# Elu features of four blocks read from the transposed q, and the order of issue written anew

## The chip, the core and the metric

The program runs on one core of a Trainium2 chip. Its time is the time of one execution on the device, in microseconds (us); the kernel before was run three times, and the median is the figure that a changed kernel is compared with. One further execution of the same program was taken by the hardware profiler; all rows below come from that one.

The engines of the core work side by side, each on its own list of instructions: PE (TensorE: matrix products, and transposes as products with the identity matrix), ACT (ScalarE), DVE (VectorE), POOL (GpSimd) and SP (SyncE, which here only issues transfers). An instruction starts when the one ahead of it on its engine is through and the data, the buffers and the transfers that it waits for are there.

## The reference

The computation is an attention with a memory branch, followed by a gated feed-forward layer:

```
scores = q k^T / sqrt(D), causal;  a = softmax(scores);  local = a v
phi(x) = (x > 0 ? x : exp(x) - 1) + 1
mem    = (phi(q) M_prev) / (phi(q) z_prev + 1e-6)
x      = g * mem + (1 - g) * local,   g = sigmoid(beta), one per head
xn     = x / rms(x) * rms_g
out    = (silu(xn w_gate) * (xn w_val)) w_out
```

q, k and v have 4 batches, 8 heads, 576 rows and 64 columns; x has 2304 tokens of 512 values; the gated layer is 1536 wide. All inputs and the output are fp32.

## The kernel before, in words

The 2304 tokens are worked off as 18 blocks of 128 rows, and the gated layer takes them as 9 chunks of two blocks. Attention of later blocks runs beside the gated layer of earlier chunks, so that TensorE always has a product to do.

The first four blocks (`n < NA`, NA = 4) take an fp32 way; the others split every operand into two fp16 halves and transpose them by DMA. Only the fp32 way is touched here. For such a block, q and k are loaded as rows (tiles `q` and `kv`, 128 rows by 512 values). `prep_qk32` transposes k and q on TensorE (`transposed`, L571: four products with `ident` into the PSUM tile `tp`), and ACT copies each 128x512 result to SBUF (L573), k into `k32`, q into the half `q32[n][:, 0]`. `phi_calc` computes phi: ACT takes the exponential of q as loaded (L553), DVE takes the smaller of that and 1 (L554), and DVE takes the larger of q + 1 and that (L555). `prep_phi32` then transposes the features `ph` in the same way (four more products at L571, one ACT copy at L573 into the half `q32[n][:, 1]`). The scores are products of `k32` and `q32[n][:, 0]` (L637); `S` is their row-reduced form on DVE (L654), its exponential is on ACT (L712), and it is transposed again on TensorE before the product with v (L852). The memory branch multiplies `q32[n][:, 1]` with a matrix `Mpair` that holds M_prev and z_prev of two heads (L825).

A block's result is put together on DVE and POOL (L838, L868, L870, tile `t`). ACT sums its squares (L428, tile `junk`), POOL makes the row's scale of it (L928, L931), DVE builds a diagonal matrix (L942, `diag`), and TensorE multiplies the block with it (L947, `xtp`), which transposes and scales at once. Two blocks make the first chunk `xT`, on which the fp32 gated products (L1105) run.

Other work of the first 60 us: `csum` (L317) sums squares of k and v for the scales of the fp16 blocks, `allp` (L289) spreads a column over all partitions, and `busy` (L308) are products whose result nobody reads; eight of them open the program. The weights come as 64-bit words and are made fp32 by ACT and DVE (L1023, L1024, L1028) and then split in fp16 halves (L245 to L266).

**What sets the order.** The order of issue of every engine is written out: `ISSUE` holds one string for each of the five engines, in which a letter stands for a kind of instruction (the letter is given by `@keep`; "T" is a transposition, "f" an operation of `phi_calc`), a number behind it for a repetition, and `~` with a number for how many of the kind that are still to come are passed over. A function reads the strings and ties each instruction to the one ahead of it. The transfers of SP are in such a string too. A transfer takes one of eight lanes in turn, and waits for the transfer eight before it.

Of the kernel before, what the change touches and what calls it, by code (L numbers as in the profile page):

```python
# [90 lines left out]
        "3SG2P2SPG~1P2G~1G~1P2S~2G~1G~1G~1PS~2PS~2S~2G~1G~1PS~2G~1D~2GPSDP~1SPSGSG5SDG3D~3GPD~3GP3DPD~2S32GDPG~2PGP3GDPGP"
        "2GP2GPD~3P3G3DG6PG2D~2PGDGPDG3PG3D~1PG~1G~1G~1P3GP2GPGP2G4P2G3YG3PG2P2D~1P3GG~6GP3GDG3G~1GPD~1D2S~8S~8S~8S~8S~20"
        "S~20S~8S~8S~8S~8S~8S~8S~8S~8S~8S~8S~8S~8S~8S~8S~8S~8S~8S~8S~8S~8S~8S~8S~8S~8S~8S~8M4S8M12P2G2PG6DG3G~11G3G~8G8D~"
        "3GDG7D~2G2S27D2G2D~1GDGG~8G2G~6G4G~2GD~2G~1G~1G~1G~1D2G~1G~1G~1G~1G~1DG2D~1GDG3PS2P2SP2G3D~2GDD~1DSPS3P3SPSPSP3S"
        "PS2P45S~8S~8S~8S~8S~8S~8S~8S~8S~8S~8S~8S~8S~8S~8S~8S~9S~9S~9S~9S~9S~9S~9P3S~9P2S~9P2S~9P2S~9S~9P4S~9P2S~9PS~8PS~"
        "8P2S~8P11G3D~1D~1G9DG15D~1D~1G4DM16P29S8GD~1G4D2G16D~1G2D~1G4D~1GS~8S~8G5S7PSG5S2GSGS~3GDSG~3G~3SG~3G~3G~3G~3GG~"
        "2G~2S~1SGDSDG5D~1GDS2GDS~3DGD~3GS~3S~3SDSDGSDG~7G2G~5DG~5G~5G2G~3SG~3G~3G~3GG~2D~1GSGS2GDS~1D~2S~1G3SDGS2P120G~1"
        "0GG~9D~1G~9G3D~1D~4D~4GG~5G3G~2G~2G~2GG~1GDMGDGD~2G10SG2G~2GG~1G~1G~1SG~1MG~1GSMSDGMDG3DG2M3GMG6MGMGG~3MG~3MG2G~"
        "1PG2M2G3P2GDGP2DP3MP2GPMDP3G3PD~2GDG3DGP2DP3GPG~5D~1G~5GPG2G~2P~2P~2P~2P~2PG~2P~1G~2P~1G~2G~2P~1P~1P~1G~2GPGD~1G"
        "PG2P2DGPG3PG3D~1PG2D2PG2P2D~1PG~2PGPG7P3SD~1G3S~5G4D~1G4DGDG~5G2S~5SS~4G3S4D~2D~2GSDGS2G4DG2SG2SGDS2M2SGSDGMD~2M"  # L100
        "S2GSM~4M~4MGMSG2SGMSG2D~2SM~1GG~2M~1M~1D~2G~2G3D2MGSS~4S2G2DS~2MGS~2DGSG2S2D~1G6DSG2PGDGS~1SGPG2P2GP4GSGSPSMSMG4"
        "P5GS~1S~1PS~1PG3SGDGPD~3G7DG3PG2S~3S~3S~3G4SPS~2GS~2GS~2G2PGPSS~1PDD~1SP2GD~1PG2PGPG3P4DPGSD~3SPSG2PSDSG3P2SGSG~"
# [66 lines left out]
def attn_memory_moe_kernel(  # L169
# [1154 lines left out]
    for n in range(2):  # L1324
        prep_qk32(n)
        phi_calc(n)
        prep_phi32(n)
# [223 lines left out]
```

## Time and profile before

| What | us |
| --- | --- |
| three runs, lowest / median / highest | 584.06 / 584.78 / 584.83 |
| the profiled execution | 583.54 |
| its span (first to last instruction) | 581.8 |
| around the span | 1.74 |
| PE busy in the span | 574.0 |
| DVE / ACT / POOL busy | 424.2 / 398.3 / 131.3 |

The profiled execution is 1.24 us below the median of the three runs. The rows further down show its views: a page of shares, the waits of an engine, its busy time in stretches of the span, and timelines, where several instructions of one kind that follow each other stand in one row with their count.

### The profile page before, as it was taken

What the parts mean: (1) busy time and instruction counts of PE and PEld (TensorE: products, weight loads), DVE (VectorE), ACT (ScalarE), POOL (GpSimd) and SP (SyncE); (2) the same over time, 40 slices, a digit from 0 to 9 for tenths busy, and PEclk for the clock granted to TensorE, in tenths of its full rate; (3) what the DMA queues carried; (4) which work ended last, traced back from release to release, by engine and by line L of the source; (5) the groups of instructions that cost most, each with busy time, mean ns of one, the idle gap of its engine ahead of it and who ended that gap; (6) DMA issues with size and microseconds to landing.
All of it is one profiled execution on the core that took longest, in us unless ns stands there. A gap on an engine that the chain in (4) does not pass through costs nothing.

```text
span 581.8 us, 16060 instructions
## 1 busy us (share of the span) xinstructions
PE 574.0 (99%) x6230; PEld 454.1 (78%) x6230; DVE 424.2 (73%) x1278; ACT 398.3 (68%) x857; POOL 131.3 (23%) x219
## 2 busy tenths in 40 slices
PE   8999999999999999999999999999999999999996
PEld 8888866687777787887777778787877777777885
DVE  5898869999997878775788787988766675642221
ACT  6899888998996757665677678867655553543222
POOL 2511100053322222212213221213221211132111
PEclk9999999999999999999999999999999999999999
DMA  8999666579898778977579877597666653462001
GB/s 260 347 361 373 238 230 130 111 133 241 168 164 156 155 158 131 148 142 138 99 160 162 175 149 155 107 180 138 111 123 114 103 100 65 95 90 47 27 1 37
DMA packets 183948, 87.59 MB, mean 151 GB/s; under 512 B 165824, under 2 KB 166080, under 8 KB 183872
## 3 DMA queue, kind: packets, MB, share of 16 engines
q1 hardware_dynamic: 180800, 81.95, 66.3%
q10 hardware_dynamic: 3072, 4.61, 2.3%
q8 instruction: 49, 0.80, 0.6%
q14 instruction: 27, 0.22, 0.1%
HBM read 37.77 MB, written 4.72 MB: 73 GB/s over the span
## 4 chain that ended last, share of the span: by engine, by line
PE 93%; DMA 3%; ACT 1%; DVE 1%; issue 0%; POOL 0%; ACTq 0%; POOLq 0%
PE gv L1112 42%; PE out L1193 21%; PE gv L1105 7%; PE sc L648 5%; PE out L1182 3%; PE loc L770 2%; PE loc L771 1%; PE loc L772 1%; PE csum L317 1%; PE sc L677 1%; PE loc L788 1%; DMA kv<-in_qkv_dram 1%; PE tp L571 1%; PE mem L886 1%; DMA q<-in_qkv_dram 1%; DMA PT<-P 1%
## 5 line engine op out<-in xcount | busy, mean ns | idle before, releaser
L1112 PE MATMUL gv<-xT,wgv 128*128 128x256 f16 x2304 | 357.1, 273 | 0.0
L1112 PEld LDWEIGHTS <-wgv 128*128 128x128 f16 x2304 | 209.2, 98 | 49.9 <-issue 3.2
L1193 PE MATMUL out<-wo,h 128*128 128x512 f16 (+1 forms) x528 | 176.0, 372 | 0.0
L1151 POOL TENSOR_TENSOR h<-th,h 128x256 f16<-128x256 f32 x88 | 64.6, 735 | 275.1 <-ACT h L1150 252.5
L1129 ACT ACTIVATE th<-gv,wt 128x256 f32<-128x256 f32 x96 | 45.1, 469 | 75.5 <-PE gv L1112 70.3
L648 PE MATMUL sc<-kT,qT 128*128 128x128 f16 x576 | 95.3, 219 | 0.0
L720 ACT ACTIVATE S<-S,nm 128x384 f32<-128x384 f32 (+3 forms) x112 | 70.7, 637 | 28.3 <-DVE nm L654 16.5
L1130 DVE SCALAR_TENSOR_TENSOR th<-th,gv 128x256 f32<-128x256 f32 x96 | 40.0, 417 | 62.0 <-ACT th L1129 61.5
L739 DVE SCALAR_TENSOR_TENSOR P<-S,P 128x512 f16<-128x512 f32 (+2 forms) x96 | 65.2, 680 | 22.3 <-ACT P L219 21.4
L654 DVE CUSTOM_DVE_ANT_0 S<-sc,mask,qsc 128x256 f32<-128x256 f32 (+2 forms) x96 | 57.8, 612 | 17.7 <-PE sc L648 16.5
L1193 PEld LDWEIGHTS <-h 128*128 128x128 f16 x564 | 54.1, 98 | 14.1 <-POOL h L1151 0.5
L219 ACT ACTIVATE P<-S 128x512 f16<-128x512 f32 (+2 forms) x96 | 58.2, 607 | 8.1 <-DMA PT<-P 6.8
L648 PEld LDWEIGHTS <-qT 128*128 128x128 f16 x576 | 52.1, 98 | 10.5 <-issue 0.6
L772 PE MATMUL loc<-v,PT 128*128 128x65 f16 x288 | 53.0, 193 | 0.0
L770 PE MATMUL loc<-v,PT 128*128 128x65 f16 x288 | 52.5, 193 | 0.4 <-DMA PT<-P 0.4
L1150 ACT CAST h<-th 128x256 f16<-128x256 f32 x88 | 34.8, 396 | 26.3 <-DVE th L1133 12.1
L771 PE MATMUL loc<-v,PT 128*128 128x64 f16 x288 | 52.5, 193 | 0.0
L1133 DVE SCALAR_TENSOR_TENSOR th<-th,wt,gv 128x256 f32<-128x256 f32 x96 | 45.6, 475 | 1.6
L1105 PE MATMUL gv<-xT,wgv 128*128 128x256 f32 x192 | 46.5, 385 | 0.0
L1105 PEld LDWEIGHTS gv<-xT,wgv 128*128 128x128 f32 x192 | 35.0, 190 | 8.3 <-issue 3.6
L770 PEld LDWEIGHTS <-PT 128*128 128x128 f16 x288 | 28.1, 98 | 6.9 <-DMA PT<-P 0.7
L886 PE MATMUL mem<-M,phT 128*128 128x65 f16 (+1 forms) x256 | 32.9, 194 | 0.0
(225 smaller groups left out, 908.4 us busy)
## 6 DMA issues: line engine op xcount, KB each, us to landing
kv<-in_qkv_dram SPq DMA_DIRECT2D x40, 256.0 KB, 3.6
q<-in_qkv_dram SPq DMA_DIRECT2D x18, 256.0 KB, 3.6
wo<-in_moe_w_out_dram SPq DMA_DIRECT2D x8, 512.0 KB, 5.1
out_dram<-res ACTq DMA_DIRECT2D x16, 256.0 KB, 2.5
wgv<-in_moe_w_val_dram SPq DMA_DIRECT2D x7, 512.0 KB, 7.2
wo<-in_moe_w_gate_dram SPq DMA_DIRECT2D x7, 512.0 KB, 7.4
qT<-qT SPq DMA_DIRECT2D x28, 128.0 KB, 2.6
wgv<-in_moe_w_gate_dram SPq DMA_DIRECT2D x5, 512.0 KB, 6.1
```

Source lines behind the costliest of these rows:

```text
L219: got = fn(*p, **k)
L648: nc.tensor.matmul(t[:, g * w + j * P : g * w + (j + 1) * P], qT[n][:, t2, h, :], kT[blk_of[(b, j)]][:, h, :], start=(t2 == 0), stop=(t2 = ...
L654: nc.vector.tensor_tensor_reduce(out=s[:, g * w : (g + 1) * w], in0=t[:, g * w : (g + 1) * w], in1=mask[:, m0 : m0 + w], scale=qsc[n][:, 5 ...
L720: nc.scalar.activation(v_, v_, AF.Exp, bias=nm[:, g : g + 1], scale=-1.0)
L739: m = nc.vector.scalar_tensor_tensor(out=p16[:, w : 2 * w], in0=s[:, :w], scalar=PSCALE, in1=p16[:, :w], op0=ALU.mult, op1=ALU.subtract)
L770: nc.tensor.matmul(a, phi_, vhi, start=(j == 0), stop=False)
L771: nc.tensor.matmul(a[:, :D], phi_, vlo, start=False, stop=False)
L772: nc.tensor.matmul(a, plo, vhi, start=False, stop=(j == nb - 1))
L1105: nc.tensor.matmul(o, wgv[:, 1 + p, o0 : o0 + P], xT[0][:, cc, at], start=(cc == 0), stop=(cc == NC - 1))
L1112: nc.tensor.matmul(o, lhs, xT[c][:, rhs, :], start=(cnt == 0), stop=(cnt == 3 * NC - 1))
L1151: nc.gpsimd.tensor_tensor(h16[:, 1], th, h16[:, 0], ALU.subtract)
L1193: nc.tensor.matmul((o if half is None else o[half])[:, at], lhs, rhs[:, at], start=(f == 0 and rhs is whi and lhs is hh), stop=(f == NF - ...
```

## The change

`phi_calc` reads the transposed q that already lies in `q32[n][:, 0]` and writes the features straight into `q32[n][:, 1]`, for the first four blocks. `prep_phi32` is gone, with its transposes and copies. The other blocks compute as before. The five strings of `ISSUE` are replaced (one pair of lines shown, of some 100).

```diff
     "DVE": (
-        ".~1f2.JZI~4Z.f2S3.~1I~4SII~3.S2IS2IS3TISiS2TiSi~1Su~1uiuiu~1uTi2Iiu~1Tiuiuiu2RiR2JfZft.ZU~1RS3USf2STSu~1SI~1iuSi"
+        ".~1J.Z.2I~4fI~4ZI.fS6.SI~3fIS2IfTS3IS2i~3SiSTiu2iuiu~1uTi2Tiu3Ii3u2RiU~1R2JZtZRfS2fS3TSIS2iu~1tuiufu2Si~1SiTSifS"
...
     @keep("f")
     def phi_calc(n):
-        ph = sb.tile([P, HD], F32, tag="t2", name="ph", bufs=1)
-        nc.scalar.activation(ph, qst[n], AF.Exp)
+        if n < NA:
+            q, ph = (q32[n][:, t].rearrange("p c s -> p (c s)") for t in range(2))
+            qst.pop(n)
+        else:
+            q, ph = qst[n], sb.tile([P, HD], F32, tag="t2", name="ph", bufs=1)
+            qst[n] = ph
+        nc.scalar.activation(ph, q, AF.Exp)
         nc.vector.tensor_scalar(ph, ph, 1.0, None, op0=ALU.min)
         nc.vector.scalar_tensor_tensor(
-            out=ph, in0=qst[n], scalar=1.0, in1=ph, op0=ALU.add, op1=ALU.max
-        )
-        qst[n] = ph
+            out=ph, in0=q, scalar=1.0, in1=ph, op0=ALU.add, op1=ALU.max
+        )
...
-    @keep("n")
-    def prep_phi32(n):
-        transposed(q32[n][:, 1], qst.pop(n), T32[2] == "a")
...
-            st[4].append((0.3, lambda: prep_phi32(n)))
...
-        prep_phi32(n)
```

On ACT the program begins, before, with the small transfers, the load of the activation table and the exponential of q of block 0 as loaded (`few` and `zz` are rms_g and z_prev; `q_104`, `q_109` are q of blocks 0 and 1 as loaded, `q_0_161` and `q_1_185` their transposed tiles):

```order
L1204 DMA few<-in_moe_rms_g_dram 128x4
L1206 DMA zz<-in_z_prev_dram 64x32 x2
L553 ACT_TABLE_LOAD
L553 ACTIVATE ph<-q_104 128x512
L1203 DMA beta_sb<-in_beta_dram 128x8
L428 ACTIVATE junk,zq<-zz 128x32
L573 COPY k_0_154<-tp 128x512
L573 COPY q_0_161<-tp 128x512 x2
L553 ACTIVATE ph<-q_109 128x512
```

Now the same place reads (the numbers of lines and tiles are those of the changed kernel, in which `q_1_178` is the tile of block 1):

```order
L1205 DMA zz<-in_z_prev_dram 64x32
L1203 DMA few<-in_moe_rms_g_dram 128x4
L1205 DMA zz<-in_z_prev_dram 64x32
L1202 DMA beta_sb<-in_beta_dram 128x8
L427 ACT_TABLE_LOAD
L427 ACTIVATE junk,zq<-zz 128x32
L576 COPY k_0_154<-tp 128x512
L576 COPY q_0_161<-tp 128x512
L557 ACTIVATE q_0_161<-q_0_161 128x512
```

The exponential of block 0 has moved behind the two copies, the table load stands ahead of the sum of squares of `zz`, and of the two copies into `q_0_161` one is left.

On DVE, between the first small operations and the first reduction of scores (`S`), stood before:

```order
L293 TENSOR_REDUCE vmax<-allp 128x1
L331 MEMSET few 128x2
L554 TENSOR_SCALAR ph<-ph 128x512
L555 SCALAR_TENSOR_TENSOR ph<-q_109,ph 128x512
L654 ISA S,nm<-sc,mask 128x128
```

and ahead of these the two operations of block 0. Now there stands:

```order
L275 TENSOR_SCALAR pw<-vmax 128x1
L558 TENSOR_SCALAR q_0_161<-q_0_161 128x512
L276 TENSOR_SCALAR pw<-pw 128x1
L292 TENSOR_REDUCE vmax<-allp 128x1
L1219 TENSOR_SCALAR gsig<-gsig 128x8
L337 COPY tmask<-mask 128x128
L559 SCALAR_TENSOR_TENSOR q_0_161<-q_0_161 128x512
L653 ISA S,nm<-sc,mask 128x128
```

Block 0 has its two operations right ahead of the first reduction; those of block 1 follow behind it, between the reductions, and the copy into `tmask`, which followed the third reduction, is ahead of the first.

On PE, after the first scores, stood before:

```order
L637 MATMUL sc<-k_0_154,q_0_161 128x128 x6
L308 MATMUL busy<-ident 128x128
L571 MATMUL tp<-ident,ph 128x128 x2
L825 MATMUL mem_315<-Mpair,q_0_161 128x130
L571 MATMUL tp<-ident,ph 128x128
```

and now:

```order
L636 MATMUL sc<-k_0_154,q_0_161 128x128 x6
L316 LDWEIGHTS kv_106
L316 MATMUL csum_615<-kv_106 128x128
L316 LDWEIGHTS kv_106
L316 MATMUL csum_615<-kv_106 128x128
L824 MATMUL mem_301<-Mpair,q_0_161 128x130
```

The transposes of `ph` are gone from the list, and so is the `busy` product of this place; there are nine instead of eight at the start. All in all PE issues 16 matmuls fewer, DVE as many operations as before. From about 100 us on PE's list is nearly the same.

## Rows read from the trace of the kernel before

**Rows 1.** The page: busy time, share of the span and instructions of each engine

```profile
PE 574.0 (99%) x6230; PEld 454.1 (78%) x6230; DVE 424.2 (73%) x1278; ACT 398.3 (68%) x857; POOL 131.3 (23%) x219
```

**Rows 2.** The page: the chain that ended last, shares of the span

```profile
PE 93%; DMA 3%; ACT 1%; DVE 1%; issue 0%; POOL 0%; ACTq 0%; POOLq 0%
```

**Rows 3.** The waits of PE inside the program: total us, times, longest us

```profile
...
PE xtp L947 <- DVE few L1214: 0.7, 1, 0.7
PE allp L289 <- ACT junk L428: 0.4, 1, 0.4
PE loc L770 <- DMA PT<-P: 0.4, 1, 0.4
```

**Rows 4.** Busy us in stretches: PE, PEld, DVE, ACT, POOL, then PEclk, DMA share, GB/s

```profile
10.00:15.00 5.00, 5.00 (x42) 4.31 (x41) 4.42 (x37) 4.87 (x22) 0.89 (x3) 1.00 1.01 373
15.00:20.00 5.00, 5.00 (x49) 4.95 (x48) 4.84 (x23) 3.68 (x17) 1.50 (x3) 1.00 1.05 408
...
26.00:40.00 14.00, 13.98 (x116) 12.60 (x117) 12.70 (x58) 13.63 (x42) 3.46 (x8) 1.00 1.03 371
120.00:130.00 10.00, 10.00 (x97) 8.16 (x95) 10.00 (x35) 9.75 (x23) 6.53 (x10) 1.00 1.00 166
...
570.00:582.00 12.00, 6.97 (x54) 4.96 (x51) 2.28 (x5) 2.92 (x6) 1.62 (x3) 0.90 0.16 46
```

**Rows 5.** All instructions of line 571: ns min/median/max, first and last start in us

```profile
L571 PE MATMUL tp<-ident,ph x16: 272/273/283, 6.8 to 33.8; 128*128 128x128 f32 x16
```

**Rows 6.** Timeline of PE: start, us, line, count, and in brackets the wait ahead

```profile
1.47 3.79 PE L308 MATMUL busy<-ident 128*128 128x128 f32 x16 [1.47 <-POOL ident L325]
...
5.05 1.06 PE L571 MATMUL tp<-ident,kv 128*128 128x128 f32 x4
...
5.90 0.37 PE L571 MATMUL tp<-ident,q 128*128 128x128 f32 x1
...
26.02 1.16 PE L947 MATMUL xtp<-diag,t 128*128 128x128 f32 x8 [0.67 <-DVE few L1214]
...
27.24 0.60 PE L571 MATMUL tp<-ident,ph 128*128 128x128 f32 x4
...
27.67 0.27 PE L571 MATMUL tp<-ident,kv 128*128 128x128 f32 x1
...
32.55 0.49 PE L571 MATMUL tp<-ident,ph 128*128 128x128 f32 x3
```

**Rows 7.** ACT's copies of transposed tiles into q32, 0 to 40 us: busy us, mean ns

```profile
L573 ACT COPY q<-tp 128x512 f32<-128x512 f32 x8 | 4.6, 574 | 1.3 <-PE tp L571 1.3
```

**Rows 8.** Timeline of ACT in the head

```profile
2.46 1.28 ACT L553 ACT_TABLE_LOAD   x1 [2.46 <-issue]
4.47 0.63 ACT L553 ACTIVATE ph<-q 128x512 f32<-128x512 f32 x1 [0.73 <-DMA q<-in_qkv_dram]
...
5.42 0.23 ACT L428 ACTIVATE junk<-zz 128x32 bf16<-128x32 f32 x1 [0.32 <-DMA zz<-in_z_prev_dram]
...
6.14 0.59 ACT L573 COPY k<-tp 128x512 f32<-128x512 f32 x1 [0.40 <-PE tp L571]
```

**Rows 9.** Timeline of DVE up to the evacuation of block 1

```profile
8.69 0.43 DVE L554 TENSOR_SCALAR ph<-ph 128x512 f32<-128x512 f32 x1 [0.46 <-ACT ph L553]
9.16 0.69 DVE L555 SCALAR_TENSOR_TENSOR ph<-q,ph 128x512 f32<-128x512 f32 x1
10.24 0.29 DVE L654 CUSTOM_DVE_ANT_0 S<-sc,mask 128x128 f32<-128x128 f32 x1 [0.40 <-POOL Mpair L812]
...
10.88 0.34 DVE L338 COPY tmask<-mask 128x128 bf16<-128x128 bf16 x1
...
22.07 0.42 DVE L868 TENSOR_TENSOR t<-loc,den 128x256 f32<-128x256 f32 x1
```

**Rows 10.** Timeline of POOL: the sum that ends block 1

```profile
21.88 1.42 POOL L870 TENSOR_TENSOR t<-t,t 128x256 f32<-128x256 f32 x2 [0.44 <-DVE t L838]
```

**Rows 11.** The waits of ACT between 60 and 150 us, for one weight's transfers

```profile
ACT wo L1024 <- DMA wo<-in_moe_w_out_dram: 2.2, 2, 1.9
```

More of the change, by code (lines that the diff above doesn't have):

```diff
@@ new lines @@
+        "uT2Su~1u2h3TG2ThG2sTGs~4s~4ss~3s2s~1sTG10h2G14ZG3shs3ZG3hG2s~4s~4G2sG~1G6s~3sGss~1s6s~3s2s~1s~1ss~1s~1s~1ss~1Gs~"
+        "1s3s~4s~4s~4s~4s4G2g2g~30g~30g38G3G~3Gg3g~19g~19gg~18g~18g~18g~18g2g~16g~16g~16g~16g2g~14g~14g9g~5g~5g5ZZ~1G~2G~"
+        "2GG~1g~18g~18g7g~11g~11g~11g~11g~11g~11g10g~1g~1gZ2Gg4g~18g~18g~18g~18g~18gg~17g~17g~17gg~16g~16g~16g~16g2g~14g~"
+        "14g~14g~14g~14g~14g6g~8g51G4ZDZ~1D~1g2D~2ZD~3DG5DG2ZG3D~2D2G5D~1DG3DG2DG4DG3DG5D~1D~2G2DG4SG16S~7GS~7DSS~6DSS~5S"
+        "GS4GDG13SG5S3G2M~8M3M~5MM~4D~1MG~3M~3M~3G~3G~3MSM~2G~3GSGSG~1G~1G~1GSG2SGSM~2G8SDSMG3SGS3G10SGS3G5M~1MG4DG8SG6SG"
@@ new lines @@
+        "S3GS2G5SG7P6G~2GP3G~1P2G~1GZPGS3G2P4S2P5GS2G4P2G9PGS~1SGG~2G~2G~2SGG~1G4SG8S2G3S2GS6MS2MGP5G~4PG~4G~4MG~4M2PMSP3"
+        "G~4PG2PG~2G~2GG~1G~1G~1GMP4DP4GMP3G2PD~2G7DGD~1G2D~1DD~3GDSDD~1DMDG2MG6M2G4DS~5G2P2GPGPGP2MPGDS~5D~1PSS~4S2S~2GP"
+        "G~5P3DS~2G~5S2DGDGM2D~3G~3GMSG~2SG~2P7SG~2P2D2PSG~2PGG~1G~1G~1G~1D~1S2G~1S~1GD~1DG4D~3G3S~1S~1DSGP~1P~1SP~1SP~1G"
+        "P~1P~1P~1GP~1P~1DP~1GP~1DP~1D~2SG~1PGSP2DP6GP2DSD~2GSGD~2G2D~2G3P2GSDGD2D~2G3MD~2SMG2M2G2S~1S~1D2MS~1D~1MDG~6G~6"
+        "SMGG~5G3MSG~2G~2G~2G~2G4D~2GMD~2D~2G2MGMS2M2GS2DP3G2PMDP2D~3PG2PMP4G2P3DGPGD~2PDSPDG2D2P7MPD~2S~3PS~3S~3DS~3DSD2"
@@ new lines @@
+        "P6S~2SS~1P2SPDD~2G7SG13S~5DG4S2GSG4S~2D~1S~2D2GS~2G4P2GP3S~2PG3SD~3G4DGPSPGDD~1D~1PDG~4P4GP3S~1G~3S~1G~3G~3GG~2G"
+        "~2S~1GSG~1G~1G~1G~1G~1DG~1GPSG2S~2PGSGD~2DG4D~1SG~4G~4G~4G~4G~4G~4M2G~4GG~3MGG~2P2G~2P3MPMG~2MG~2PD~1G~2S~5G~2P3"
+        "G~2G2MPG2D~4MPGP2GP3GPSGDSDGD~2G~2SGDSGS~1GS2MG3D~1GDG3P2D~3GSPS~2P3D~3G~14S~2PGP2G4PSG~9G2MPD~3MP2G3S~1GS~1GS~1"
+        "P2DMG~2G~2MSG~2PG~2G~2G~2MG~2PG~2SDG~2G~2G~2GG~1G~1G~1PG~1DG~1G~1GMGP2MD~3GD~3P2SD~3SDPGPDGPG~1G~1PS2G~1G~1G~1G~"
+        "1G~1SDSGPGD~3GPG2S3GSG2SG2PG2PDD~2PS~1PSDPG2G~4GPG2D2GDP~2PP~1P~1S2P~1P~1P~1GSP~1G3PS2GS3G2S2G5DD~1G3PGPG4S2D~1D"
@@ new lines @@
+        "~4G2D~4G2DG2DG~8G~8GG~7GG~6GG~5G~5GG~4G~4G~4GDGD~2GD~1D~6G~1G2DD~2D~2DG3D~2G2D~2GDG~7G~7GDG~6G~6GD~3D2G~5G~5GG~4"
+        "G~4GG~3D~3GG~2D~1G~2D~1G~2GD~1GD~1G11D2G5D~2G2DD~3D~3DG4DG4D~1DG~10G10D2D~1D~1DD~1D~1G5DG4DG6D~3GDG~7G~7D~2DG2G~"
+        "5G2D~1G4D2G2D~2G8G~10GG~9G~9D~2G~9G~9GG~8G~8GG~7G~7G~7G~7GG~6D2G~6G2G~4G~4G~4DG~4G~4D~6G~4G6DD~2D2D~2D~2D3G3D~2G"
+        "3DG10DD~5G~11D~5G~11DG~11GD~1G~10GG~9G5G~4G~4GG~3DG~3G~3G~3D~3D~2G~3G~3GG~2G2DG10D~6D~6D2D~4D~1D2D~1D~1D3D~2D~2D"
+        "~3DD~2D~1D~5D~1D~4DD~4D~4D~4D~3D3"
@@ L158 @@
     ),
     "SP": (
[L160 to L163 removed]
+        "blml2bm2W~1ml~2lWbd2lW~4dd~1W~7bW~4d~1d2a4W2dWl~1W~1lWW~2lW~1Wa4WW~2W3W~2B~6WW~1blW2B~2WB~1B4XB3XbB2rkr~1rkbkFrk"
@@ L164 @@
+        "r2l~1L2lbFll~1L2rl~1Lr2kLll~1L2FXLlLlbrlL2Xr2kL2FL2rl2L2bLr2LkXLlLlFLbLrL2rLXLrlkL2FL3lLrLbXL2m~1r~1rl~1lkLmLFL4"
+        "XrLr~1rkl~1lkL4bFLl2L2bLrkl2r~1rXFbrLXLr2kLlLlm2LFL5bL3XrL2k2r2LbFr3kL2XFL4rLbLr~1rLkLXL2FrLrL2XrL3kL2FL8X2D2"
     ),
```

152 lines of the change are left out of this document (64 added, 88 removed).

## The prediction

> **What bounds the kernel now.** I read the page's shares first. PE is busy 574.0 of 581.8 us [rows 1], and the chain that ended last is PE for 93% [rows 2]; so time goes only where PE has less to do or waits less. Of the 7.8 us in which PE is idle, about 1.5 lie ahead of its first product [rows 6] and 5.0 in the last 12 us, which the change does not touch (12.00 less 6.97) [rows 4]. Between these, the waits of PE leave 1.5 us: 0.7 and 0.4 just ahead of `xtp` of block 1, and 0.4 in the middle of the program [rows 3]. The reader is to see two stretches. Up to `xtp` of block 1 at 26.02 the head is a chain through several engines, whose end PE awaits; behind it PE is full (13.98 of 14.00) [rows 4], and what is taken off PE there comes off the end.
>
> **What is removed.** Sixteen transposes of `ph` go [rows 5]. A record lasts 273 ns, but that is a latency: four of them began at 27.24 and the next product at 27.67 [rows 6], so each takes 0.43 / 4 = 0.108 us of PE. In the head the pace is half that: four transposes of k began at 5.05 and the next at 5.90, 0.213 each [rows 6], but there PE also awaits what it transposes. All sixteen are worth 16 x 0.108 = 1.73 us if PE waits nowhere for anything else. The Trainium skill, "TensorE: Matmul & The Clock Gate", Part 4, gives about 275 ns for a transpose in a kernel's context and says it does not keep the clock up as a product does; its 275 ns is the trace's record of 273, but the trace's spacing of 108 ns says that they overlap, and the clock granted beside them is 1.00 [rows 4], the higher level of 2.4 GHz. By the rule's price taken in full the sum would have 4.4 us in this place.
>
> Eight of the sixteen (four at 27.24, three at 32.55, the last at 33.8) stand behind `xtp` [rows 5, 6], where PE is full: 8 x 0.108 = **-0.86**.
>
> The four copies into `q32` that go are 4 x 574 ns = 2.3 us of ACT [rows 7]. Two lie between 26 and 40 us, where ACT is busy 13.63 of 14.00, but PE there awaits nothing [rows 4], so I take 0 for them; their worth is bounded by 0 and the 0.4 us that PE waits at a later place for a transfer that ACT's work precedes [rows 3].
>
> **The ninth filler.** One `busy` product goes from about 10 us to the start. Eight of them take 3.79 us, 0.47 each [rows 6]. Where it stood it took PE's time too, so its move costs between 0 and 0.47. Ahead of the first transpose PE would wait for k anyway, so I stay near the lower end: **+0.06**.
>
> **The head, up to `xtp` of block 1.** Here the other eight transposes go, and the features are moved behind the transposed q. Before, the table load ran from 2.46 for 1.28 us, under the wait for q; the exponential began at 4.47, the sum of squares of `zz` at 5.42 when `zz` landed, and the copy of k at 6.14 [rows 8]. Now the sum of squares is the first that needs the table, and the load stands behind the same wait: about 5.35 + 1.28 = 6.63, then the sum of squares (0.32 to the next instruction) to 6.95. So the copy of k begins at 6.95, 0.8 later than before; copy of q at 7.5, exponential 8.0 to 8.6 (0.63 [rows 8]), and DVE's two operations (0.43 + 0.69 [rows 9]), with three small ones between them, to about 10.2. The wait at the load holds ACT's queue: the copies of k and q behind it, so the first scores on PE, so the first reduction on DVE. That reduction began at 10.24 before, 0.40 after DVE's list ahead of it was through, a wait that the row puts down to POOL's copies into `Mpair` [rows 9]; now I get 10.3. The slip of the copies is hidden because two of DVE's operations, block 1's (0.43 + 0.69 = 1.12), no longer stand ahead of it.
>
> The Trainium skill, "ScalarE: Activation LUTs", "What ACT_TABLE_LOAD costs", adds a drain of about 1380 ns to a load of 1283. The trace has the load at 1.28, and the exponential started 0.73 after it, at the landing of q [rows 8], so a drain of 1.38 is not seen. By the rule the copies would begin 1.4 later still, and the head would lose what the sum has it gain.
>
> Those 1.12 us of block 1 now lie among the reductions, and the copy of `tmask` (0.34) leaves [rows 9]: DVE has 0.78 us more to do between 10.24 and the evacuation of block 1, which ended at 22.07 + 0.42 = 22.49 [rows 9]. Its idle time there is 0.58 in 10 to 15 us and 0.16 in 15 to 20 [rows 4], 0.74 together. From 22.49 to `xtp` at 26.02 it is 3.5 us over POOL's sum (to 23.30 [rows 10]), ACT, POOL and DVE, all of them untouched. What PE's side gives: PE is busy 5.00 of 5.00 in both stretches [rows 4], so with its eight transposes gone (0.86) it hands scores and transposes to DVE earlier.
>
> The bounds for `xtp` of block 1: if DVE's added work comes on top of everything, 0.78 later; if PE sets the pace and its 0.86 is passed on, and the two waits of 0.4 and 0.7 go as well, 0.86 + 1.1 = 1.96 earlier. PE and DVE are both nearly full here, so neither is the whole truth. If only one of the two paces counts at a time, the middle of 0 (added work just fills the idle) and -0.86 is the nearest to both rows: **-0.4**.
>
> **The sum.** -0.86 + 0.06 - 0.4 = -1.2 us. The profiled execution took 583.54, which would become 582.3; it lies 1.24 below the median of the runs, 584.78, which becomes **583.6**. (About 0.2%, 1.17 us, is what a measurement of this kernel can tell from no change; this forecast stands on that border.)
>
> **The rivals.**
>
> *The head gives everything.* PE's eight transposes in the head come off in full, and the waits of 0.4 and 0.7 go as far as the new order lets `xtp` come earlier. For it: PE is at 5.00 of 5.00 from 10 to 20 us. Against it: both waits end on ACT, POOL and DVE [rows 3], whose work is not less. -1.7 (all transposes) to -2.8 (with both waits): 583.1 to 582.0, about 582.4.
>
> *The head swallows it.* DVE's added 0.78 us is on the path, `xtp` is 0.8 later, and the 0.86 behind it only makes up for that: -0.1, so 584.7. For it: DVE is at 4.84 of 5.00 from 15 to 20 us [rows 4]. Against it: it has 0.74 of idle time to take it up. A table load with a drain would lead to the same place.
>
> *Slower, in the weights' stretch.* SP's list of transfers is new as well, and a transfer waits for the one eight before it. DVE is busy 10.00 of 10.00 us between 120 and 130, ACT 9.75 [rows 4], and PE already waits 0.4 for a transfer of P behind it [rows 3]. ACT once waited 1.9 us for a weight `wo` in 60 to 150 us [rows 11]. If one more such weight lands late by as much, ACT's conversion and then DVE's full list slip by 1.9, and what was gained ahead is awaited away: +1.9, 586.7. It decides from the point where the weight is later than ACT's 0.25 us of slack in that stretch. Against it: from 100 us on the order is nearly as before, and a head that is earlier gives the transfers no less time.
>
> *Transposes at their full latency.* If TensorE did nothing else beside them, 16 x 0.273 = 4.4 us go: 580.4. Against it is the spacing of 0.108; for it only the 0.213 of the head. The page of the Trainium skill named above (TensorE, Part 4) speaks for this one.
>
> That the change doesn't do what it says I see no room for: the transposes are gone from PE's list.
>
> **How the numbers follow.** The forecast (its own range 582.9 to 584.2) has 0.45, half of it over the border of 0.2% and half within. The head gives everything: 0.22; it swallows: 0.22; slower in the weights' stretch: 0.09; full latency: 0.02. Faster by over 0.2% is then 0.23 + 0.22 + 0.02 = 0.47, within 0.2% is 0.22 + 0.22 = 0.44, and slower 0.09. The range 582.0 to 585.3 leaves out the last two rivals and allows for half a microsecond on the one that swallows.
>
> **What would show it.** Right: 64 records of `tp` on PE and four copies of q and four of k on ACT; the table load at about 5.3 and the copy of k at 6.9; the first reduction of scores at 10.2 to 10.4; `xtp` of block 1 at 25.3 to 25.9, and what follows it (the first fp32 gated products) earlier by 1.0 to 1.4; the same 0.4 us wait of PE for P near 130 us, or a longer one. The forecast is wrong in the head if `xtp` comes at 26.5 or later, or at 24.5 or before; it is wrong later if PE shows a new wait behind 60 us of more than half a microsecond, and its end is then to be read from what that wait ends on.

## The result: slower, 588.77 us for 584.81

The changed kernel takes 588.77 us (median of 4 runs, 588.05 to 589.61), the kernel before, measured beside it, 584.81 (584.06 to 585.02): ratio 1.0065 [1.0052, 1.0078], 4.0 us slower. The forecast was 583.6, its range ended at 585.3. The two profiled executions stand 5.3 us apart in time and span (588.82 and 587.1, for 583.54 and 581.8). Some runs of these kernels show a lower granted clock and are several us longer; the ratios leave out the two longest (595.55 in h2, 595.77 in f4, of the table below) and hold the others.

The changed kernel's page, first the shares and then the chain that ended last:

```profile
PE 575.1 (98%) x6214; PEld 452.3 (77%) x6214; DVE 425.6 (72%) x1278; ACT 397.3 (68%) x853; POOL 126.5 (22%) x219
...
PE 78%; DVE 12%; DMA 5%; ACT 2%; issue 2%; POOL 0%; ACTq 0%; DVEq 0%; POOLq 0%
```

The 16 matmuls are gone, but DVE, 1% of the chain before [rows 2], is now 12% of it. The waits of PE in the changed kernel (total us, times, longest):

```profile
PE allp L288 <- ACT junk L427: 1.5, 2, 1.3
...
PE gv L1111 <- DVE th L1132: 1.3, 1, 1.3
PE xtp L946 <- DVE few L1213: 0.7, 1, 0.7
PE loc L769 <- DMA PT<-P: 0.6, 1, 0.6
```

Against [rows 3] two are new in size: 1.3 us in the head, at the sum of squares of `zz`, and 1.3 at a gated product that awaits DVE's `th`. The second stands at 129 us, a hundred microseconds behind everything that the edit of the features touches (the order of issue is new there too). The wait for `PT`, P as a transfer transposes it, is new in place: 0.56 us at 173 us, where the kernel before waits 0.43 at 132. The stretches show it (busy us of PE, PEld, DVE, ACT, POOL; PEclk, DMA share, GB/s), before:

```profile
120.00:150.00 30.00, 29.57 (x326) 24.13 (x324) 29.77 (x98) 27.68 (x59) 14.57 (x24) 1.00 0.96 198
150.00:180.00 30.00, 30.00 (x325) 22.38 (x323) 29.26 (x84) 27.15 (x57) 8.22 (x11) 1.00 0.90 162
```

and after:

```profile
120.00:150.00 30.00, 28.03 (x302) 22.63 (x300) 29.96 (x92) 25.95 (x56) 11.94 (x17) 1.00 0.86 170
150.00:180.00 30.00, 29.29 (x312) 21.17 (x309) 28.77 (x79) 27.11 (x58) 7.60 (x12) 1.00 0.88 165
```

In the first stretch DVE is busier than before (29.96) and yet gets through fewer instructions: 92 for 98. So some of them last longer. DVE's timeline in the changed kernel, with the two POOL operations that matter:

```profile
126.57 1.16 POOL L268 TENSOR_TENSOR wgv<-wgv 128x512 f16<-128x512 f32 x1 [3.44 <-ACT wgv L265]
126.61 1.67 DVE L738 SCALAR_TENSOR_TENSOR P<-S,P 128x512 f16<-128x512 f32 x1
...
137.82 1.16 POOL L268 TENSOR_TENSOR wgv<-wgv 128x512 f16<-128x512 f32 x1 [0.20 <-ACT wgv L265]
138.35 0.65 DVE L279 TENSOR_SCALAR qsc<-pw 128x2 f32<-128x2 f32 x1
```

And before, the same instructions:

```profile
125.18 0.68 DVE L739 SCALAR_TENSOR_TENSOR P<-S,P 128x512 f16<-128x512 f32 x1
125.30 1.57 POOL L269 TENSOR_TENSOR wgv<-wgv 128x512 f16<-128x512 f32 x1 [3.32 <-ACT wgv L266]
...
135.30 0.14 DVE L280 TENSOR_SCALAR qsc<-pw 128x2 f32<-128x2 f32 x1
135.34 1.16 POOL L269 TENSOR_TENSOR wgv<-wgv 128x512 f16<-128x512 f32 x1
```

`P` takes 0.68 us where it starts 0.12 before POOL's operation, which then takes 1.57 for 1.16; it takes 1.67 where it starts 0.04 behind it. An operation on 128x2 elements goes from 0.14 to 0.65. In these pairs whoever starts second waits out the first. No wait of PE behind 60 us ends on POOL in the changed kernel; DVE is full, and there it costs time. I call the sum over DVE's instructions between 110 and 160 us of what each lasts beyond the median of its operation and operands (where over 0.12 us) the *stretch*: 0.36 us before, 3.27 after, from 6 instructions. The Trainium skill, "GPSIMD Engine Reference" (specifications), says that GpSimd shares SBUF interfaces with VectorE and contends with its instructions that have two SBUF inputs or are in a two-port mode; `P`, with two operands in SBUF, is such a case, and the trace agrees that they collide.

The other new wait is in the head. ACT, DVE and PE in the changed kernel:

```profile
6.21 1.28 ACT L427 ACT_TABLE_LOAD   x1 [6.21 <-DMA zz<-in_z_prev_dram]
7.50 0.23 ACT L427 ACTIVATE junk<-zz 128x32 bf16<-128x32 f32 x1
7.73 0.57 ACT L576 COPY k<-tp 128x512 f32<-128x512 f32 x1
7.88 0.49 PE L288 MATMUL allp<-ident,zq 128*128 128x128 f32 x2 [1.30 <-ACT junk L427]
11.11 0.29 DVE L653 CUSTOM_DVE_ANT_0 S<-sc,mask 128x128 f32<-128x128 f32 x1
27.33 0.94 PE L946 MATMUL xtp<-diag,t 128*128 128x128 f32 x6 [0.72 <-DVE few L1213]
```

The load does wait for `zz`, as forecast, but `zz` landed at 6.13 us and not at 5.34: SP now issues the first transfer of `M_prev` 2.2 us earlier (1.70 for 3.93), and `zz`, issued at 2.02, lands 0.17 behind it.

To tell where time is lost I use one mark: the 193rd gated product (`gv`) on PE, up to which both programs issue the same ones. It starts at 107.9 us before and at 108.7 after, so 0.8 of the 5.3 us of the profiled pair is lost ahead of it and **4.5 behind it**.

### The profile page after: what moved, and what is told of

The parts are those of the page before. It is cut to its first block, busy times and chain, and to the rows that moved or that the text cites. A ratio compares the mean times of both kernels' runs of the same rounds, so it can differ in the third digit from the quotient of the medians.

```text
span 587.1 us, 16001 instructions
## 1 busy us (share of the span) xinstructions
PE 575.1 (98%) x6214; PEld 452.3 (77%) x6214; DVE 425.6 (72%) x1278; ACT 397.3 (68%) x853; POOL 126.5 (22%) x219
## 4 chain that ended last, share of the span: by engine, by line
PE 78%; DVE 12%; DMA 5%; ACT 2%; issue 2%; POOL 0%; ACTq 0%; DVEq 0%; POOLq 0%
PE gv L1111 37%; PE out L1192 18%; PE gv L1104 5%; PE sc L647 4%; DMA PT<-P 3%; DVE S L653 2%; PE csum L316 1%; PE sc L676 1%; PE loc L787 1%; PE loc L769 1%; DVE wgv L247 1%; PE loc L770 1%; DVE P L738 1%; PE loc L771 1%; PE loc L851 1%
## 5 line engine op out<-in xcount | busy, mean ns | idle before, releaser
L1192 PE MATMUL out<-wo,h 128*128 128x512 f16 (+1 forms) x528 | 173.7, 372 | 0.0
L719 ACT ACTIVATE S<-S,nm 128x256 f32<-128x256 f32 (+3 forms) x112 | 70.6, 640 | 38.4 <-DVE nm L653 25.9
L647 PE MATMUL sc<-kT,qT 128*128 128x128 f16 x576 | 94.1, 219 | 0.3 <-DVE nm L653 0.3
```

Of the source, the lines that this page charges most:

```text
L647: nc.tensor.matmul(t[:, g * w + j * P : g * w + (j + 1) * P], qT[n][:, t2, h, :], kT[blk_of[(b, j)]][:, h, :], start=(t2 == 0), stop=(t2 = ...
L719: nc.scalar.activation(v_, v_, AF.Exp, bias=nm[:, g : g + 1], scale=-1.0)
L1192: nc.tensor.matmul((o if half is None else o[half])[:, at], lhs, rhs[:, at], start=(f == 0 and rhs is whi and lhs is hh), stop=(f == NF - ...
```

## The experiments

The theories: *A*, the head (the table load behind `zz`) makes the kernel slower; *B*, the new order of issue between 105 and 200 us does; and within B, *B1*, DVE's instructions that fall behind POOL's, or something else of the order. Each table row gives the median, the ratio to the kernel before that was measured beside it, and from the profiled execution its time, the start of the mark, the lag gathered behind it (mark to end, less 473.9 of before), the stretch, and the time from the 421st to the 601st gated product, which lie at 153 and 194 us in the kernel before.

```
run                    us      ratio [95%]              profile mark   lag   stretch 421-601
after                  588.77  1.0065 [1.0052, 1.0078]  588.82  108.7  +4.5  3.27  42.73
e1_early_table         587.61  1.0037 [1.0019, 1.0055]  585.92  107.9  +2.3  1.80  42.61
e2_square_first        590.02  1.0095 [1.0057, 1.0134]  586.51  110.0  +0.8  1.60  40.93
e3_edit_alone          590.06  1.0086 [1.0072, 1.0100]  591.03  113.2  +2.2  1.60  40.93
e4_thin_before         585.93  1.0012 [1.0001, 1.0022]  586.04  108.6  +1.8  0.00  40.93
e4_thin_after          587.17  1.0045 [1.0024, 1.0066]  589.27  110.0  +3.6  0.00  42.43
h1_tail_before         586.92  1.0051 [1.0021, 1.0081]  589.67  111.9  +2.1  1.60  40.94
h2_tail_before_early   586.01  1.0021 [1.0012, 1.0030]  586.02  108.6  +1.8  1.60  40.94
f1_M_back              587.40  1.0041 [1.0028, 1.0054]  588.56  108.0  +4.9  3.22  42.93
f2_M_back_early        588.08  1.0055 [1.0043, 1.0067]  588.40  108.0  +4.8  3.21  42.98
f3_M_back_early_tail   586.68  1.0041 [1.0021, 1.0061]  588.42  110.4  +2.3  1.61  40.94
f4_tail160_before      589.02  1.0059 [1.0040, 1.0078]  589.72  109.2  +4.9  3.23  41.92
g1_swaps               586.46  1.0017 [1.0008, 1.0026]  586.53  108.3  +2.6  0.40  42.09
g2_after_swaps         586.43  1.0026 [1.0015, 1.0037]  588.87  111.0  +2.3  0.41  42.60
g3_best                584.94  1.0005 [0.9994, 1.0017]  584.73  108.3  +0.8  0.77  40.94
g4_k1_early            585.21  0.9999 [0.9989, 1.0009]  585.21  107.9  +1.7  0.78  40.94
```

The profiled execution is one of several, and its time can stand 3.5 us from the median. In those of h1, f3, g2 and e3 the granted clock fell to 0.50 ahead of the mark, so their marks are late by that as well; lags are counted from the mark.

**The table load taken from behind `zz`.** In the changed kernel one more exponential of a column stands ahead of it on ACT:

```
+        early = tiny.tile([P, 1], F32, tag="early", name="early", bufs=1)
+        keep("*")(nc.scalar.activation)(early, ident[:, 0:1], AF.Exp)
```

> The changed kernel with one more instruction: ACT takes the exponential of one column of the identity matrix right behind its four small transfers, so that the activation table is loaded at about 3 us and no longer behind the landing of z_prev at 6.2. Theory H (the head: the load behind z_prev makes the copy of k, the first reduction and all of DVE's list late, and the stretch in which DVE is full, 90 to 160 us, hands it on): copy of k at about 6.5 in place of 7.73, first reduction of scores at 10.0 to 10.3 in place of 11.11, xtp of block 1 at 26.0 to 26.5 in place of 27.3, and 1.0 to 1.7 us less in all, about 587.4. Theory C (DVE's instructions of 110 to 160 us are stretched where a POOL instruction starts just ahead of them, 3.3 us in the changed kernel against 0.4 before): the head comes earlier as H says, but the time follows the stretching, which the shift deals anew: between 583.5 (none left) and 588 (all left). Rival R (the new order between 26 and 120 us is what costs): head earlier, time within 0.5 us of the changed kernel's 588.8.

The load went to 3.23 us, the copy of k to 6.42, the first reduction to 10.41, the mark to 107.9, level with before. The kernel gained 1.2 us of the 4.0 in its median; it stayed slower. Its lag also fell, to 2.3, though nothing of the order behind 105 us had been touched: an earlier head shifts when DVE and POOL meet, and in the profiled execution fewer met (it is a short one: 585.92, of runs from 585.76 to 588.55).

**The reverse: the kernel before with the square of `zz` ahead of its exponential** (ACT's list):

```
-L553 ACT_TABLE_LOAD
+L428 ACT_TABLE_LOAD
+L428 ACTIVATE junk,zq<-zz 128x32
 L553 ACTIVATE ph<-q_104 128x512
 L1203 DMA beta_sb<-in_beta_dram 128x8
-L428 ACTIVATE junk,zq<-zz 128x32
```

> The kernel before with one instruction of ACT moved: the sum of squares of z_prev goes ahead of the exponential of block 0, so that here too the table load waits for z_prev. All else is as before, the sixteen transposes too. Theory H: the load starts at 5.4 in place of 2.46, the exponential at about 7.0 in place of 4.47, the copy of k at about 7.6 in place of 6.14, the first reduction 1.0 to 1.5 later than 10.24, and 1.0 to 1.7 us more in all, about 586.1. Theory C: the same start, and on top of it up to 3 us where the shift lets POOL's instructions start ahead of DVE's in 110 to 160 us: 586 to 589. Rival R: the head's slip is taken up by PE's idle time and DVE's waits before 60 us, within 0.4 us of 584.8.

The head lost 2.1 us (first reduction 12.41, mark 110.0), more than the changed kernel's 0.8. The runs spread from 586.5 to 595.0: in four of the six the mean granted clock was 0.984 to 0.993, in the other two (586.51 and 588.40) 0.998 or more. So the median is no price of a late load; by these two it is 1.5 to 3.4 us.

**The edit in the order of before**, with the early load:

> The edit of the features alone, in the order of the kernel before: the sixteen transposes and four copies are taken out of the lists of PE and ACT, the operations of the features stand at the first place behind the copy of q that they now need, and the table is loaded early by an exponential of one column in the place of block 0's. POOL's and SP's lists are those of before. Theory H: no late load, so the head isn't late (first reduction at 9.9 to 10.4, xtp of block 1 at 25.3 to 26.5) and the time is at or under the kernel before's: 583.5 to 584.8. Theory C: the same, and up to 3 us more if POOL comes first in 110 to 160 us. Rival E (the edit itself costs, because the features follow the copies and their DVE operations come among the reductions): first reduction on time, xtp of block 1 later than 26.5, and 1 us or more above 584.8.

Inconclusive for the edit. The head was early (reduction 10.07, `xtp` of block 1 at 25.81), but PE then waited 1.0 us at 36 us for `den` of DVE, and behind it the granted clock fell to its lower level:

```profile
34.00:38.00 4.00, 2.97 (x23) 2.47 (x23) 3.66 (x23) 3.59 (x14) 0.59 (x1) 0.94 1.01 393
38.00:42.00 4.00, 4.00 (x20) 3.77 (x21) 2.07 (x9) 2.88 (x12) 0.00 (x0) 0.50 0.91 353
```

PEclk is 0.50 from 38 to 42 us, that is 1.2 GHz, behind the stretch in which PE was busy 2.97 of 4.00. All five runs have a mean clock of 0.992 or 0.993. The slow clock and the awaited DVE together put the mark 5.3 us late. In the order of before, then, the edit itself makes a wait ahead of 40 us; what it does in a fitting order these runs must tell.

**POOL's part made thin.** The low halves that POOL writes are cut to 16 columns, in before and after alike (ACT's copy writes both halves; so the low halves are not computed):

```
+            nc.scalar.copy(h16, th.unsqueeze(1).to_broadcast([P, 2, 2 * P]))
+            nc.gpsimd.tensor_tensor(h16[:, 1, :16], th[:, :16], h16[:, 0, :16], ALU.subtract)
```

> The kernel before with POOL's share of the splits made thin: in 5 splits of weights and the 8 splits of h16e, POOL computes 16 columns of the low half, and ACT's copy, which writes the high half, writes both halves. The low halves are left out of the result so. POOL then has no long instruction between 110 and 160 us that could start ahead of one of DVE's. It is the partner of the next run. Theory C (POOL's instructions stretch DVE's): little to gain here, as only 0.36 us of stretching was seen: within 1 us of 585.0. Theory O (the order of DVE's list behind 105 us): the same.

> The changed kernel with the same thin splits (the low halves of 5 splits of weights and of the 8 splits of h16e are left out of the result). Theory C: the 3.3 us of stretched DVE instructions between 110 and 160 us go, and the changed kernel stands 1.0 to 1.8 us above its thin partner (the late head alone) instead of 4. Theory O: the stretching was not what cost; it stands 3 to 4.5 us above its thin partner as without the thinning.

POOL's operation then takes 0.22 us:

```profile
129.34 0.22 POOL L270 TENSOR_TENSOR wgv<-wgv 128x16 f16<-128x16 f32 x1 [4.91 <-ACT wgv L265]
```

The stretch is 0.00 in both, and the gap of the medians is 1.24 us instead of 3.96 (1.9 by the ratios). So some half of the loss or more needs POOL's long operations. The thinning is not free itself: with it the kernel before takes 1.1 us more. The two profiled executions are 3.2 us apart: 1.4 at the mark, 0.4 more up to the 421st gated product, where the changed kernel had lost 2.7, and 1.5 from there to the 601st.

**The order of before behind 105 us**, the changed kernel's ahead of it, without and with the early load:

> The changed kernel with the order of before behind 105 us: what each engine had issued in the kernel before by 105 us comes first, in the order that the changed kernel gives it, and all the rest follows in the order of the kernel before. The late table load stays. Theory O: only the late head is left, 1.0 to 1.7 us above before: 586.0 to 586.8. Theory C: the head's delay stays, and POOL and DVE meet as it falls: 586 to 589, with stretched DVE instructions of more than 1 us in 110 to 160 us where it is above 587. Theory H in its strong form (the late head alone makes all of the 4 us): 588 to 589.

> The same as the last one with the table loaded early, as in the run that loaded it behind ACT's small transfers (587.6). Theory O: nothing of the 4 us is left, and what PE is spared behind the first chunk's xtp shows: 584.0 to 585.2. Theory C: 584 to 588, by how much DVE is stretched between 110 and 160 us. If it is 587 or more with little stretching, the loss lies in the order between 26 and 105 us.

The lag fell from 4.5 to about 2, the stretch to 1.6; with the early load as well the kernel stood 1.2 us over before. By the medians and the lags the order behind 105 us thus has a large part of the loss, though not all; the ratio of h1 is too wide to tell. Even with before's own order there, operations meet, since the head brings DVE and POOL to it at other times. In this variant:

```profile
136.08 1.16 POOL L260 TENSOR_TENSOR wgv<-wgv 128x512 f16<-128x512 f32 x1 [0.19 <-ACT wgv L257]
136.39 0.92 DVE L271 TENSOR_SCALAR qsc<-pw 128x2 f32<-128x2 f32 x1
```

Two elements in each partition, 0.92 us.

**`M_prev` back behind k and q of block 1 on SP**, and three more from there: with the early load, with the order of before behind 105 us, and (without the early load) with it only behind 160 us:

> The changed kernel with SP's first eight transfers in another order: k and q of block 1 ahead of the first part of M_prev, as before. Theory M (the transfer of M_prev, issued at 1.70 us just ahead of the second half of z_prev at 2.02, holds z_prev back: both land together, at 5.96 and 6.13 in the changed kernel, at 6.6 to 6.9 in three variants, while z_prev lands at 5.34 to 5.50 where M_prev is issued after it): z_prev lands at 5.3 to 5.5, the table load starts then, the copy of k at about 6.9 in place of 7.73, the first reduction at 10.2 to 10.5 in place of 11.11, and 0.6 to 1.2 us less in all, about 587.9. Rival D (z_prev is late because it is issued third on ACT, not because of M_prev): z_prev at 6.0 or later, no gain in the head, 588.3 to 589.2.

> The last one with the early table load as well. Theory M: the head is then as early as the kernel before's: copy of k at 6.0 to 6.2, first reduction at 9.7 to 10.2, xtp of block 1 at 25.4 to 26.0; 586.5 to 587.2 in all, since what the order behind 105 us costs (1.7 by the two runs that put it back) stays. If it comes to 585 or less, the order behind 105 us costs only with a late head.

> The last one with the order of before behind 105 us as well: all three suspects are undone, the edit of the features and the order of the first 105 us are left. Theories M and O together: 583.9 to 585.0, at or below the kernel before, with PE's first f16 gated products 0.3 to 0.8 us earlier than before's. Theory C (DVE is stretched by POOL as soon as anything shifts): first gated products earlier as said, and yet 585.3 to 586.5, with 1.2 us or more of stretched DVE instructions between 110 and 160 us.

> The changed kernel with the order of before behind 160 us only; up to there its own order, the late head included. With the order put back behind 105 us the time was 586.9. If what the tail's order costs lies between 105 and 160 us, where DVE is full (theory O): 588.3 to 589.2, as the changed kernel. If it lies behind 160 us: 586.5 to 587.4.

In the first `zz` landed at 5.60 us for 6.13, and the mark went to 108.0. The second is the sharpest against A: its head is healed, the mark at 108.0 is level with before, and it still takes 588.08. All its loss lies behind the mark, a lag of 4.8 at a stretch of 3.21, and the wait of a gated product for `th` is there again (1.4 us). Its stretches:

```profile
110.00:130.00 20.00, 18.57 (x162) 13.87 (x161) 19.96 (x58) 18.00 (x38) 5.79 (x8) 1.00 0.51 104
130.00:160.00 30.00, 29.21 (x334) 22.86 (x332) 29.93 (x89) 25.56 (x52) 10.00 (x18) 1.00 0.86 179
160.00:200.00 40.00, 38.83 (x413) 29.37 (x412) 34.54 (x99) 31.77 (x68) 10.10 (x15) 1.00 0.86 165
```

PE idles 3.4 us in these 90, and DVE is full in the first 50 of them (19.96 of 20.00, 29.93 of 30.00). The fourth, with the order of before only behind 160 us, changed nothing in the time (lag 4.9). Of this lag 3.0 us are there by the 421st gated product, at 157 us, under its own order; the rest comes behind it all the same, so the run does not say that the order there is free. The third came out near h2, 2.0 us over before and so above both of its forecasts.

**Five changes of place in DVE's list between 125 and 157 us, and nothing else**, on the second of these (g1) and on the changed kernel itself (g2). Two of the five:

```
+L738 SCALAR_TENSOR_TENSOR P_1605<-S,P_1605 128x512
 L1129 SCALAR_TENSOR_TENSOR th<-th,gv_1587 128x256
-L738 SCALAR_TENSOR_TENSOR P_1605<-S,P_1605 128x512
...
+L1129 SCALAR_TENSOR_TENSOR th<-th,gv_2348 128x256
 L247 SCALAR_TENSOR_TENSOR wo<-wo,wos 128x512
-L1129 SCALAR_TENSOR_TENSOR th<-th,gv_2348 128x256
```

> The kernel with M_prev's transfer put back and the early table load (588.1, PE level with the kernel before at its first f16 gated products, 3.2 us of stretched DVE instructions in 110 to 160 us), and in DVE's list five small changes of places between 125 and 157 us, in which an instruction that was stretched goes ahead of, or behind, one or two neighbours that run beside POOL without stretching, so that it starts before POOL's instruction or after its end. No work is changed. Theory C: the stretching falls from 3.2 to under 1.5 us, and the time by 1.5 to 3 us, to 585.1 to 586.6. Rival S (the stretching does not matter, DVE has other slack): within 0.6 us of 588.1.

> The changed kernel itself with the same five changes of places in DVE's list, the late head left as it is. Theory C: 585.8 to 587.3 in place of 588.8, stretching under 1.5 us. Rival S: 588.2 to 589.4.

This is the test of B1. No work, engine or transfer changes, only places in DVE's list, chosen so that an instruction starts before POOL's or behind it. A place is also a turn, and a part of the gain may be that: `th` now comes ahead of a `wo` of 1.25 us. These two runs do not part the two; the thin runs, which move nothing in DVE's list, have the stretch alone gone, at the price named. In g2:

```profile
127.63 0.69 DVE L738 SCALAR_TENSOR_TENSOR P<-S,P 128x512 f16<-128x512 f32 x1
128.00 1.33 POOL L268 TENSOR_TENSOR wgv<-wgv 128x512 f16<-128x512 f32 x1 [3.52 <-ACT wgv L265]
...
130.03 0.74 DVE L247 SCALAR_TENSOR_TENSOR row<-ph,qsc,row 128x512 f16<-128x512 f32 x1
130.63 0.68 POOL L1150 TENSOR_TENSOR h16e<-th,h16e 128x256 f16<-128x256 f32 x1 [0.66 <-ACT h16e L1149]
```

`P` is back at 0.69, `row` at 0.74 (1.21 in the changed kernel), POOL's operation is the longer one. The changed kernel went from 588.77 to 586.43, by 2.3 us; f2 went from 588.08 to 586.46, by 1.6.

The lag that is left, 2.3 us in g2, can be placed. Up to the 421st gated product it is 0.7 (2.7 in the changed kernel); from there to the 601st it grows by 1.7. That piece lasts 40.93 or 40.94 us in all nine executions that have before's order there, and 42.09 to 42.98 in all seven that have the changed one, whatever the head and the stretch ahead (last column; f4, whose order changes within it, has 41.92). The engines there, in the kernel before, in g1 and in g4 (stretch 0.40 and 0.78):

```profile
160.00:200.00 40.00, 40.00 (x438) 31.09 (x437) 34.40 (x94) 32.24 (x71) 10.83 (x17) 1.00 0.88 159
160.00:200.00 40.00, 39.36 (x424) 30.25 (x423) 34.44 (x95) 32.53 (x72) 10.48 (x16) 1.00 0.85 168
160.00:200.00 40.00, 40.00 (x431) 30.68 (x429) 34.71 (x97) 32.38 (x71) 11.46 (x17) 1.00 0.78 157
```

What PE waits for there is a transfer of P, and it waits for one in each of the seven and in none of the nine. In g2 (whole program):

```profile
PE loc L769 <- DMA PT<-P: 1.0, 2, 0.8
```

So B holds with both of its parts: DVE behind POOL up to about 155 us, and another cost of the new order from there to about 195. Which place in the lists makes that transfer late no run has tried.

**The best that I could put together**: the changed kernel's order up to 105 us, the early load, both halves of `zz` first on ACT's queue, before's order behind 105, and the small operations on `pw` and `qsc` earlier (g3); then also the k of block 1 third on SP, ahead of `M_prev` (g4):

```
-L383 DMA wo<-in_M_prev_dram 64x512
+L372 DMA kv_113<-in_qkv_dram 128x512
 L372 DMA kv_108<-in_qkv_dram 128x512
-L372 DMA kv_113<-in_qkv_dram 128x512
 L414 DMA q_111<-in_qkv_dram 128x512
-L383 DMA wo<-in_M_prev_dram 64x512 x2
+L383 DMA wo<-in_M_prev_dram 64x512 x3
```

> An attempt to have the edit without its cost: the changed kernel's order of the first 105 us with the table loaded early, both halves of z_prev issued first on ACT, the order of before behind 105 us (586.0 with the early table), and there the two operations on the scale of q (pw, qsc) two and five places earlier in DVE's list, ahead of POOL's instruction that stretched them by 1.25 us. Theory C: stretching 0.4 to 0.8 us and 583.9 to 585.0, at or just below the kernel before's 584.8. Rival S: 585.6 to 586.5.

> The last attempt (584.9, level with the kernel before) with one more change: SP issues k of block 1 third, then v of block 0, q of block 1 and only then M_prev, in place of M_prev third. There the head waited 1.2 us at 8.2 for k of block 1, which landed at 8.09. Expected: k of block 1 lands at about 5.7, the first reduction of scores comes at 9.3 to 9.9 in place of 10.85, xtp of block 1 at 25.3 to 26.0 in place of 26.9, PE's first f16 gated products at 107.0 to 107.6 in place of 108.3. Theory C: whether this reaches the end depends on what the shift does to DVE and POOL in 110 to 160 us: 583.8 to 584.6 if the stretching stays at 0.8 us, 585.0 to 586.5 if it is 1.5 us or more. If the head alone counted it would be 584.0.

Both measure as before does: 1.0005 [0.9994, 1.0017] and 0.9999 [0.9989, 1.0009]. g4 missed its forecast: its first reduction came at 10.29 and `xtp` of block 1 at 26.36, both later than expected, and at a stretch of 0.78 it was to take 584.6 or less. g4's 120 to 180 us:

```profile
120.00:150.00 30.00, 29.20 (x316) 23.45 (x315) 29.86 (x96) 27.03 (x58) 14.21 (x24) 1.00 0.88 187
150.00:180.00 30.00, 30.00 (x321) 22.36 (x319) 29.36 (x84) 26.89 (x58) 8.05 (x11) 1.00 0.85 157
```

DVE is at 96 instructions of before's 98, and still full. Sixteen transposes fewer on PE gained nothing that can be measured, with most of the new costs gone. No version beat the kernel before.

## Why the prediction was wrong

**What was right.** The counts: 64 records of `tp`, and four copies each of q and k:

```profile
L576 ACT COPY k<-tp 128x512 f32<-128x512 f32 x4 | 2.3, 575 | 0.0
L576 ACT COPY q<-tp 128x512 f32<-128x512 f32 x4 | 2.3, 576 | 0.8 <-PE tp L574 0.8
```

The load now stands ahead of the sum of squares, waits for `zz` and holds the copies of k and q; it takes 1.28 us and the next instruction follows at once, with no drain to be seen. Of the rival with transposes at full latency no run shows a trace.

**The step that failed: "behind it PE is full (13.98 of 14.00), and what is taken off PE there comes off the end".** I read a busy share of PE from 26 to 40 us as the bound of the end. What decides lies further on, where the same group of rows showed DVE at 10.00 of 10.00 [rows 4]: behind the mark the changed kernel loses 4.5 us, 1.25 of them in one wait of PE for DVE's `th`. Nor did the term of -0.86 come through in full ahead of that. From `xtp` of block 1 to the mark PE has the eight transposes and one `csum` product less, and takes 81.37 us for 81.87 before: 0.5 (0.3 in g4). g4 has the mark level with before, `xtp` of block 1 only 0.34 us later and sixteen transposes less, and gains nothing: behind the mark it falls back by 1.7. Of that PE idles 0.4, and the same instructions keep it busy 1.3 longer. That DVE, nearly full there, is what holds it is my reading; no run makes DVE's work less.

**The head, -0.4.** Its first line took the landing of `zz` as 5.35 from the trace of before, while the same diff moved `M_prev` ahead of it on SP: 6.13. So the first reduction came at 11.11 instead of 10.3, and `xtp` of block 1 at 27.33 instead of 25.6. But the term was wrong apart from that: with the load early (e1: 26.57), with `zz` early as well (f2: 26.59) or k too (g4: 26.36), `xtp` came no earlier in the changed kernel's order than in before. The rival "the head swallows it" had the balance right, a later `xtp` made up for by the mark. That it is DVE's added 0.78 which lies on the path no run shows by itself.

**The rival on the slower side** had the right place (120 to 130 us, DVE full) and the wrong cause. ACT's longest wait for a weight between 60 and 200 us is 1.4 us, under the 1.9 of before. What PE awaits at 129 us is DVE's `th`, queued behind a `P` of 1.67 us. I gave it 0.09 and argued that "from 100 us on the order is nearly as before"; nearly the same order, come to at another time, was enough (e1 against the changed kernel: one list behind 105 us, stretch 1.80 and 3.27).

**The account of the 4.0 us.** In the profiled pair, 5.3 us apart, 0.8 lie ahead of the mark, 2.7 between it and the 421st gated product, and 1.8 from there to the 601st; behind that nothing more is lost. Five places in DVE's list take 2.0 of the 2.7 away (g2), and 2.3 of the median. POOL made thin leaves a gap of 1.24 to 1.9 between the two orders, so by it 2.1 to 2.7 hang on POOL's operations. About half of the loss or somewhat more is thus DVE waiting out POOL, and most of the rest is the new order from 155 to 195 us, where PE waits for a transfer of P; the late head has the smallest part. A late load was worth 1.2 in e1, part of it by fewer meetings, so these terms cannot simply be added. What stays open: why PE, beside its waits, is busy longer with the same instructions from 155 to 195 us (41.6 us for 40.9 in g2). And variants whose lists differ little move by 0.7 us (f1 and f2, h2 and f3), so differences under a microsecond between two variants are not read here.

## What to carry to other kernels

Before work taken off an engine is counted as time, look along the whole span for the stretch where another engine is full, for that stretch can take the gain back; here it was a hundred microseconds behind the edit. Where two engines are tuned to run without meeting, any shift ahead of them is a cost of unknown size with more ways to lose than to gain, and the chance of "slower" must hold it. And when an order of issue is new, take the landing time of each transfer in the sum anew: a small transfer can be held by the one issued ahead of it.

## What the runs showed of the hardware

- DVE and POOL take turns on some operations, and the one that starts first goes first. Behind a POOL tensor operation of 1.16 us, `P` (fp16 out, two operands in SBUF) took 1.67 us for 0.69, and a 128x2 operation 0.92 for 0.14. Where they started first, `P` kept its time and POOL's took 1.33 and 1.57. Counted over five profiled executions (before, after, h2, f2, g2), where a DVE instruction began within a POOL operation of over 0.6 us that had 0.25 us or more to go: `wgv` (128x512, int32) was longer by over 0.1 us in 9 of 9, `x` in 5 of 5, the fp16 `v` in 16 of 16, `P` of 128x512 in 13 of 13; the fp32 `th` in 0 of 158 and the reductions S in 0 of 135.
- A transfer of 8 KB (`zz`) landed 0.2 us behind the larger one that another engine had issued 0.3 us ahead of it: at 6.13 us, `M_prev` at 5.96; e1 has 5.81 behind 5.63, h2 6.95 behind 6.78. In g2 it came at 7.08, 1.6 behind `M_prev`, so that is not all that holds it. Where `M_prev` was issued later it came at 5.34 (before), 5.33 (g1), 5.60 (f1), 5.64 (f2) and 6.02 (f3). The Trainium skill, "DMA: Bandwidth & Descriptors" (issuing engines are not separate DMA queues), says that the transfers of all issuing engines share the 16 DMA engines; the trace agrees.
- The granted clock fell to 0.50 ahead of the mark in four of the profiled executions: for 6.8 us from 8.3 in h1, for 3.4 from 10.1 in g2 and from 10.3 in f3, and for 6.8 from 37.5 in e3. In h1 PE was busy 2.30 of the 4.30 us ahead of the fall. In e3 PE was busy 6.85 of the 8 us from 26 to 34 and 2.97 of the next 4. In before, after, e1, e2, f1, f2 and g4 it was 1.00 from 4 to 105 us.
